# Moving transposes from TensorE to the DMA engines, with fills and port order, in a linear-attention and Fourier-mixing kernel

## The chip, the cores and the metric

One core of one Trainium2 chip runs the whole program. The metric is device time in microseconds (us), the median of several executions. An execution counts as slow when it is over 1.5% above the fastest of the same kernel. The median and the range that are given first are of all four executions; where some of the four were slow, the median of the fast ones stands beside them and is the one that is compared. Engines are called TensorE (PE in the profile), ScalarE (ACT), VectorE (DVE), GpSimd (POOL) and SyncE (SP); "PEld" is TensorE's weight load.

## The reference, cut to what matters

```python
# r, k, v, w: [4, 8, 768, 48]; u: [8, 48]; w_ch1: [384, 1536]; w_ch2: [1536, 384]; all float32
for t in range(S):                                    # recurrence over 768 steps, 8 heads
    cur = einsum('bhd,bhe->bhde', u * k_t, v_t)
    y_t = einsum('bhd,bhde->bhe', r_t, state + cur)
    state = w_t[..., None] * state + einsum('bhd,bhe->bhde', k_t, v_t)
x = y as [4, 768, 384]
u_ = x + real(fft(fft(x, axis=1), axis=2))            # Fourier mixing
un = (u_ - mean) / sqrt(var + 1e-6)
out = u_ + maximum(un @ w_ch1, 0) @ w_ch2             # MLP
```

## The kernel before

The recurrence is worked out in chunks of 128 steps: 6 chunks for each of 4 batches, so 24 chunks. In a chunk, r and k are scaled by decay factors (`rh`, `kh`, rows = time) and are then transposed (`rT`, `kT`, rows = channels), which is the form in which the matmuls that follow, which sum over channels, take them. After the Fourier mixing the normed rows `un` are transposed (`unt`) for the MLP.

```python
        # in attention(b, c), for each of 24 chunks
        def tr_r(e):
            for h in range(H):                                   # 8 heads
                o0 = 128 * h - 64 * (h % 2)
                ins = e.transpose(psb(trr)[:, 128 * h:128 * h + 128], rflat[:, o0:o0 + 128], IDB[:, :])
            return ins
        op("pe", 450, tr_r, r=["IDB", ("RH", i2)], w=[trr])
        # ... the same for k, 4 transposes ...
        op("act", 1000, lambda e: e.activation(rT[:, :, :].rearrange("p h t -> p (h t)"), psb(trr)[:, :], ACTF.Copy),
           r=[trr], w=[("RTB", i2)])
        op("act", 570, lambda e: e.activation(kT[:, :, :].rearrange("p h t -> p (h t)"), psb(trk)[:, 0:512], ACTF.Copy),
           r=[trk], w=[("KTB", i2)])
        # ... in mix(b), for each of 24 blocks of normed rows
            op("act", 600, act(un[:, :], uf[:, kb, :], ACTF.Identity, scale=-1.0, bias=agg[:, kb, 0:1]), ...)
            def tr(e, un=un, tu=tu):
                for m in range(NM):                              # 3 tiles; NIDW is the negative identity
                    ins = e.matmul(ps(tu)[:, 128 * m:128 * m + 128], un[:, 128 * m:128 * m + 128], NIDW[:, 128:256])
                return ins
            op("pe", 168, tr, r=["NIDW", ("UN", n % 3)], w=[tu])
            op("act", 475, ...)                                  # eviction of tu into unt
        # ... weights of the MLP, on GpSimd's queue
            op("pool", 1000, lambda e, q=q: e.dma_start(W1[:, q, :], moe_w_ch1[q * 128:(q + 1) * 128, :]), ...)   # x3
            op("pool", 1000, lambda e, q=q: e.dma_start(W2[:, 4 * q:4 * q + 4, :], ...), ...)                      # x3
```

`op(engine, ns, f, r=, w=)` records an operation with a cost estimate. `schedule()` is a list scheduler in Python: it simulates the engines with these estimates and priority keys (the constants `A0, AP, F0, ...`, "the plan" below) and fixes each engine's order. The program gives each engine its instructions in this order, each preceded by waits for the semaphores of what it needs, and what stands behind a held instruction waits too: in `after_wlate` below, ScalarE did nothing for 13.4 us behind two issues. So a change of an estimate, or of the work on one engine, can move instructions on all of them.

## Time and profile before

| | before |
|---|---|
| time, median of 4 (in the rounds with the kernel after) | 220.97 us (220.22 to 222.15) |
| busy over the span of 219.5 us: TensorE / VectorE / ScalarE / GpSimd | 196.0 / 155.1 / 153.0 / 119.4 us |
| mean granted TensorE clock | 0.982 |

The next fence has lines of the profile's page of the kernel before: busy time by engine; the span in 40 slices of 5.5 us (busy tenths, the granted TensorE clock in tenths, the DMA engines' busy share); the chain of work that ended last, by engine and by line; and three groups of instructions (busy us, mean ns of one, idle time before them and what ended it).

```profile
PE 196.0 (89%) x1838; PEld 130.4 (59%) x1838; DVE 155.1 (71%) x317; ACT 153.0 (70%) x322; POOL 119.4 (54%) x152
...
PE   0165798989969999999999999999999999999993
...
ACT  2349758969689885468988975689899246773330
...
PEclk9999679999999999999999999999999999999998
DMA  5999999999999999601938981015001010111102
...
PE 79%; DVE 13%; ACT 6%; issue 1%; DVEq 0%
...
L573 ACT ACTIVATE rtb<-bank 128x1024 bf16<-128x1024 bf16 x24 | 24.6, 1026 | 9.2 <-PE bank L564 8.9
...
L564 PE MATMUL bank<-idw,rh 128*128 128x128 bf16 x192 | 15.1, 223 | 5.5 <-DVE rh L552 5.5
L575 ACT ACTIVATE ktb<-bank 128x512 bf16<-128x512 bf16 x24 | 14.3, 597 | 6.0 <-PE bank L570 5.8
```

How to read it: TensorE is full from slice 13 on (from 66 us), 79% of the chain is TensorE's, and ScalarE's digits are mostly 6 to 9 up to slice 31. So TensorE bounds the kernel, with ScalarE not far behind. The DMA engines are full in the first 16 slices (some 88 us), where the inputs and weights are loaded. L573, L575 and L683 (489 ns, 24 times) are the evictions of transposes that the change removes (of L573 and L575, 18 of the 24). The view by stretch gives the numbers for the stretch that matters, 46 to 192 us (the columns are busy us and, in brackets, instructions by engine, then clock, DMA share and GB/s):

```profile
core 0: us, PE busy (x) PEld busy (x) DVE busy (x) ACT busy (x) POOL busy (x), PEclk, DMA share, GB/s
46.00:192.00 146.00, 143.60 (x1432) 98.58 (x1433) 109.54 (x234) 112.92 (x243) 85.56 (x103) 1.00 0.52 109
```

### The profile page before, as it was taken

How to read it: one execution, taken by the hardware profiler on the slowest of the kernel's cores; microseconds unless marked ns; L12 is line 12 of the kernel's file. 1: busy time of each engine (PE TensorE's matmuls, PEld its weight loads, DVE VectorE, ACT ScalarE, POOL GpSimd, SP SyncE). 2: the span in 40 equal slices, each digit the busy share in tenths (PEclk: the TensorE clock that was granted, in tenths of full speed). 3: DMA queues.
4: the chain of work that ended last, by engine and by line, in shares of the span. 5: the costliest groups of instructions: out<-in, count | busy, mean ns of one | idle time of the engine just before them, and what ended most of it. 6: DMA issues, size and time to landing. Idle time of an engine off the chain costs nothing.

```text
span 219.5 us, 4738 instructions
## 1 busy us (share of the span) xinstructions
PE 196.0 (89%) x1838; PEld 130.4 (59%) x1838; DVE 155.1 (71%) x317; ACT 153.0 (70%) x322; POOL 119.4 (54%) x152
## 2 busy tenths in 40 slices
PE   0165798989969999999999999999999999999993
PEld 0043455566637767566777776667777756656661
DVE  8967869997889886397587983975897818622322
ACT  2349758969689885468988975689899246773330
POOL 8818849787959898831389998103754130000000
PEclk9999679999999999999999999999999999999998
DMA  5999999999999999601938981015001010111102
GB/s 117 207 213 216 218 184 220 188 206 185 172 203 180 198 188 219 136 0 47 218 67 161 215 198 37 0 41 141 3 0 39 36 40 0 43 66 39 72 18 90
DMA packets 105478, 26.45 MB, mean 120 GB/s; under 512 B 100336, under 2 KB 105072, under 8 KB 105456
## 3 DMA queue, kind: packets, MB, share of 16 engines
q1 hardware_dynamic: 103440, 23.80, 51.0%
q0 software_dynamic: 2016, 2.36, 6.5%
q8 instruction: 14, 0.23, 0.4%
q14 instruction: 8, 0.07, 0.1%
HBM read 23.79 MB, written 4.72 MB: 130 GB/s over the span
## 4 chain that ended last, share of the span: by engine, by line
PE 79%; DVE 13%; ACT 6%; issue 1%; DVEq 0%
PE bank L702 21%; PE bank L721 21%; PE bank L645 7%; PE bank L661 5%; PE bank L564 4%; PE bank L583 4%; DVE xf L378 2%; DVE msk L382 2%; PE bank L612 2%; PE bank L678 2%; PE bank L570 2%; DVE ah L587 2%; PE bank L524 2%; PE bank L615 2%; PE bank L526 1%; PE bank L759 1%
## 5 line engine op out<-in xcount | busy, mean ns | idle before, releaser
L702 PE MATMUL bank<-unt,w 128*128 128x384 bf16 x288 | 56.5, 325 | 0.1
L721 PE MATMUL bank<-w,ht 128*128 128x384 bf16 x288 | 53.5, 326 | 0.0
L711 ACT ACTIVATE ht<-bank 128x384 bf16<-128x384 f32 x80 | 37.7, 499 | 19.3 <-PE bank L702 19.1
L587 DVE TENSOR_TENSOR ah<-bank,msk 128x512 bf16<-128x512 f32 x48 | 31.1, 682 | 8.3 <-PE bank L583 8.3
L721 PEld LDWEIGHTS bank<-w,ht 128*128 128x128 bf16 x288 | 26.7, 98 | 14.9 <-ACT unt L683 0.3
L702 PEld LDWEIGHTS bank<-unt,w 128*128 128x128 bf16 x288 | 26.3, 97 | 14.8 <-issue 0.2
L573 ACT ACTIVATE rtb<-bank 128x1024 bf16<-128x1024 bf16 x24 | 24.6, 1026 | 9.2 <-PE bank L564 8.9
L378 POOL TENSOR_TENSOR vtd<-in_v,dc 128x384 f32<-128x384 f32 x24 | 20.3, 848 | 16.7 <-DVE dc L544 16.7
L726 DVE SCALAR_TENSOR_TENSOR osb<-bank,rstd,uf 128x384 f32<-128x384 f32 x24 | 14.7, 614 | 18.4 <-PE bank L721 18.4
L378 POOL TENSOR_TENSOR rk<-in_r,in_k 128x384 f32<-128x384 f32 x24 | 24.4, 1020 | 0.8 <-DMA in_r<-in_r_dram 0.8
L378 POOL TENSOR_TENSOR rk<-rk,ub 128x384 f32<-128x384 f32 x24 | 24.7, 1028 | 0.2
L663 DVE TENSOR_TENSOR uf<-bank,x 128x384 f32<-128x384 f32 x24 | 12.3, 542 | 11.7 <-PE bank L661 11.7
L564 PE MATMUL bank<-idw,rh 128*128 128x128 bf16 x192 | 15.1, 223 | 5.5 <-DVE rh L552 5.5
L575 ACT ACTIVATE ktb<-bank 128x512 bf16<-128x512 bf16 x24 | 14.3, 597 | 6.0 <-PE bank L570 5.8
L378 POOL TENSOR_TENSOR xf<-x 128x191 bf16<-128x191 f32 x18 | 11.6, 644 | 12.5 <-DVE x L620 12.3
L620 DVE TENSOR_TENSOR x<-bank,vtd 128x384 f32<-128x384 f32 x24 | 13.3, 556 | 6.5 <-PE bank L615 4.6
L378 DVE TENSOR_TENSOR xf<-x 128x192 bf16<-128x192 f32 (+1 forms) x30 | 17.1, 584 | 0.2
L564 PEld LDWEIGHTS bank<-idw,rh 128*128 128x128 bf16 x192 | 12.4, 99 | 7.2 <-DVE rh L552 5.6
L612 PE MATMUL bank<-vb,ah 128*128 128x48 bf16 x192 | 15.2, 185 | 0.8 <-DVE ah L587 0.8
L583 PE MATMUL bank<-rtb,ktb 128*128 128x256 bf16 x96 | 15.4, 282 | 0.5 <-DVE ah L587 0.3
L612 PEld LDWEIGHTS bank<-vb,ah 128*128 128x128 bf16 x192 | 12.9, 97 | 4.7 <-DVE ah L587 1.8
L378 POOL TENSOR_TENSOR kh<-in_k,e_0 128x384 bf16<-128x384 f32 x8 | 8.1, 1016 | 13.6 <-ACT e_0 L537 13.6
(101 smaller groups left out, 402.0 us busy)
## 6 DMA issues: line engine op xcount, KB each, us to landing
in_w<-in_w_dram SPq DMA_DIRECT2D x24, 192.0 KB, 3.7
in_k<-in_k_dram SPq DMA_DIRECT2D x24, 192.0 KB, 3.9
in_r<-in_r_dram SPq DMA_DIRECT2D x24, 192.0 KB, 3.7
in_v<-in_v_dram SPq DMA_DIRECT2D x24, 192.0 KB, 3.7
out_dram<-osb SPq DMA_DIRECT2D x24, 192.0 KB, 1.9
w<-in_moe_w_ch_dram POOLq DMA_DIRECT2D x6, 384.0 KB, 8.2
ub<-in_u_dram SPq DMA_DIRECT2D x1, 192.0 KB, 3.7
```

The source lines that it names most:

```text
L378: return lambda e: e.tensor_tensor(out=o, in0=a, in1=b, op=f)
L564: ins = e.transpose(psb(trr)[:, 128 * h:128 * h + 128], rflat[:, o0:o0 + 128], IDB[:, :])
L573: op("act", 1000, lambda e: e.activation(rT[:, :, :].rearrange("p h t -> p (h t)"), psb(trr)[:, :], ACTF.Copy), r=[trr], w=[("RTB", i2)])
L575: op("act", 570, lambda e: e.activation(kT[:, :, :].rearrange("p h t -> p (h t)"), psb(trk)[:, 0:512], ACTF.Copy), r=[trk], w=[("KTB", i2)])
L583: ins = e.matmul(ps(ta)[:, 256 * x:256 * x + 256], kT[:, q, :], rT[:, 2 * q:2 * q + 2, :].rearrange("p h t -> p (h t)"))
L587: op("dve", 660, lambda e, hf=hf, ta=ta: e.tensor_tensor(out=ah[:, 4 * hf:4 * hf + 4, :], in0=ps(ta)[:, :].rearrange("p (h t) -> p h t", t ...
L612: ins = e.matmul(ps(ty)[:, D * h:D * h + D], ah[:, h, :], vb[:, h, :], start=True, stop=first)
L645: return e.matmul(ps(t)[:, 0:HF], xf[:, s, off:off + 128], tab[:, s, :], start=a, stop=z)
L702: ins = e.matmul(ps(t)[:, 0:384], W1[:, m, 128 * j:128 * j + 128], unt[:, m, :], start=(m == 0), stop=(m == NM - 1))
L711: op("act", 475, lambda e, j=j, t=t, ht=ht: e.activation(ht[:, j, :], ps(t)[:, 0:384], ACTF.Relu), r=[t], w=[("HT", q % 2, j)])
L721: ins = e.matmul(ps(t)[:, 0:DM], ht[:, j, 128 * x:128 * x + 128], W2[:, j, :], start=(j == 0), stop=(j == NJ - 1))
L726: op("dve", 610, lambda e, kb=kb, t=t, o=o: e.scalar_tensor_tensor(out=o[:, :], in0=ps(t)[:, 0:DM], scalar=rstd[:, kb:kb + 1], in1=uf[:, k ...
```

## The change

The intent is to relieve TensorE of work that is not arithmetic. From the second batch on, `rh` and `kh`, and in all batches the normed rows, are transposed by DMA from SBUF to SBUF, issued from ScalarE's queue: 18 + 18 + 24 = 60 issues. It also takes the fills off GpSimd, makes the scheduler assume one port for VectorE and GpSimd, sets a new plan, and negates W1 once instead of transposing with a negative identity.

```diff
-    A0, AP, F0, FL, M0, ML, P, KT, KW = 46.4, 4.2, 27.3, 10.5, 48.1, 44.3, 46.2, 26.7, 29.4
+    A0, AP, F0, FL, M0, ML, P, KT, KW = 46.1, 4.9, 47.0, 11.8, 54.9, 46.6, 36.0, 5.0, 41.9      # and XB = 1
 # scheduler: one port is assumed for GpSimd and some of VectorE's operations; a transfer from ScalarE's queue is
 # taken to hold the queue for 60 ns and to land after twice its bytes
+                    if o.port:
+                        s = max(s, port_t)
+            if o.bytes and e == "act":
+                dma_t = max(dma_t, s) + o.bytes / 200.0
+                o.end = s + o.dur + 2.0 * o.bytes / 200.0 + self.DMA_FIX
 # fills (cut)
-        op("pool", 1000, fill(RH[1][:, :, :], 0.0), w=[("RH", 1)])        # ... and seven more on GpSimd
+            zero([("RH", i)], RH[i].rearrange("p a b -> p (a b)"), 512)   # ... on ScalarE; others on VectorE
 # r and k
-        op("pe", 450, tr_r, ...)   op("pe", 225, tr_k, ...)   op("act", 1000, ...)   op("act", 570, ...)
+        if b >= XB:
+            op("act", 60, lambda e: e.dma_start_transpose(rT[:, :, :], rflat), r=[("RH", i2)], w=[("RTB", i2)],
+               sem="rT%d" % i2, nbytes=128 * 1024 * 2)
+            op("act", 60, lambda e: e.dma_start_transpose(kT[:, :, :], kflat), r=[("KH", i2)], w=[("KTB", i2)],
+               sem="kT%d" % i2, nbytes=128 * 512 * 2)
+        else:                      # batch 0 as before
 # normed rows
-            op("pe", 168, tr, r=["NIDW", ("UN", n % 3)], w=[tu])          # and the eviction on ScalarE
+            op("act", 60, lambda e, kb=kb, un=un, unt=unt: e.dma_start_transpose(
+                unt[:, :, 128 * (kb % 3):128 * (kb % 3) + 128], un[:, :]), ...)
 # weights
+        for q in range(NM):
+            op("dve", 500, ts(W1[:, q, :], W1[:, q, :], -1.0, None, ALU.mult), r=[("W1", q)], w=[("W1", q)])
 # ... other cuts: cost estimates of VectorE operations, the layout of rh, a wait that orders chunks
```

More of the change, by code (lines that the diff above doesn't have):

```diff
@@ L30 @@
     __slots__ = ("eng", "fn", "deps", "users", "dur", "key", "tile", "opens", "sem", "inc", "val",
-                 "start", "end", "nd", "idx", "clk", "bytes", "order", "waits", "ready", "last", "ready0")
+                 "start", "end", "nd", "idx", "clk", "bytes", "order", "waits", "ready", "last", "ready0", "port")
     def __init__(self, eng, fn, dur, key):
@@ L72, in op @@
         o.ready0 = 0.0
+        o.port = eng == "pool" and sem is None or getattr(fn, "port", False)
         for x in r:
@@ L107, in schedule @@
         dma_t = 0.0
+        port_t = 0.0
         for o in self.ops:
@@ L143, in schedule @@
             engt[e] = s + o.dur
-            if o.bytes:
+            if o.port:
+                port_t = s + o.dur
+            if o.bytes and e == "act":
+                dma_t = max(dma_t, s) + o.bytes / 200.0
+                o.end = s + o.dur + 2.0 * o.bytes / 200.0 + self.DMA_FIX
+            elif o.bytes:
                 dma_t = max(dma_t, s + o.dur) + o.bytes / 200.0
@@ L308, in sb @@
         return nc.alloc_sbuf_tensor(name, [128] + list(shape), dt).ap()
+    W0, WP, NW, XB = 8.0, 1.6, 24, 1
+    A0, AP, F0, FL, M0, ML, P, KT, KW = 46.1, 4.9, 47.0, 11.8, 54.9, 46.6, 36.0, 5.0, 41.9
     NIN = 5
@@ L375, in psb, with shared @@
         return BANK[t.bank].bitcast(BF16)
+    def shared(f):
+        f.port = True
+        return f
     def tt(o, a, b, f):
-        return lambda e: e.tensor_tensor(out=o, in0=a, in1=b, op=f)
+        return shared(lambda e: e.tensor_tensor(out=o, in0=a, in1=b, op=f))
     def ts(o, a, s1, s2, f0, f1=None):
         if f1 is None:
-            return lambda e: e.tensor_scalar(out=o, in0=a, scalar1=s1, scalar2=None, op0=f0)
-        return lambda e: e.tensor_scalar(out=o, in0=a, scalar1=s1, scalar2=s2, op0=f0, op1=f1)
+            return shared(lambda e: e.tensor_scalar(out=o, in0=a, scalar1=s1, scalar2=None, op0=f0))
+        return shared(lambda e: e.tensor_scalar(out=o, in0=a, scalar1=s1, scalar2=s2, op0=f0, op1=f1))
     def stt(o, a, s, b, f0, f1):
-        return lambda e: e.scalar_tensor_tensor(out=o, in0=a, scalar=s, in1=b, op0=f0, op1=f1)
+        return shared(lambda e: e.scalar_tensor_tensor(out=o, in0=a, scalar=s, in1=b, op0=f0, op1=f1))
     def fill(o, val):
@@ L420, in small_constants, with zero @@
         op("dve", 210, ts(NLE[:, :], CI[:, 128:256], 0.0, -1.0, ALU.is_ge, ALU.mult), r=["CI"], w=["NLE"])
-        op("dve", 400, ts(IDW[:, :], CI[:, :], 0.0, None, ALU.is_equal), r=["CI"], w=["IDB"])
-        op("dve", 270, fill(LB[1][:, :, :], 0.0), w=[("LB", 1)])
-        op("dve", 270, fill(LB[2][:, :, :], 0.0), w=[("LB", 2)])
-        op("pool", 580, fill(KH[0][:, :, :], 0.0), w=[("KH", 0)])
-        op("pool", 1000, fill(RH[1][:, :, :], 0.0), w=[("RH", 1)])
-        op("pool", 580, fill(KH[1][:, :, :], 0.0), w=[("KH", 1)])
-        op("pool", 1000, fill(RH[2][:, :, :], 0.0), w=[("RH", 2)])
-        op("pool", 580, fill(KH[2][:, :, :], 0.0), w=[("KH", 2)])
+        op("dve", 270, ts(IDW[:, :], CI[:, :], 0.0, None, ALU.is_equal), r=["CI"], w=["IDB"])
+        op("dve", 270, fill(KH[0][:, :, :], 0.0), w=[("KH", 0)])
+        def zero(res, flat, n):
+            op("act", 150 + n / 1.2, lambda e: e.activation(flat.bitcast(FP32), CI[:, 0:1].to_broadcast([128, n]),
+                                                            ACTF.Copy, scale=0.0), r=["CI"], w=res)
+        for i in range(1, NB):
+            zero([("LB", i)], LB[i].rearrange("p a b -> p (a b)"), 256)
+            zero([("RH", i)], RH[i].rearrange("p a b -> p (a b)"), 512)
+            zero([("KH", i)], KH[i].rearrange("p a b -> p (a b)"), 256)
         for i in range(2):
-            op("pool", 400, fill(XF[i][:, :, 0:64], 0.0), w=[("XFz", i)] + [("XFn", i)], key=i)
-            op("pool", 400, fill(XF[i][:, :, 446:512], 0.0), w=[("XFz2", i)] + [("XFo", i, c) for c in range(NC)], key=i)
-            op("pool", 120, fill(X[i][:, :, DM:DM + 4], 0.0), w=[("X", i, c) for c in range(NC)], key=i)
+            op("dve", 400, fill(XF[i][:, :, 0:64], 0.0), w=[("XFz", i)] + [("XFn", i)], key=2.0 + 20 * i)
+            op("dve", 400, fill(XF[i][:, :, 446:512], 0.0), w=[("XFz2", i)] + [("XFo", i, c) for c in range(NC)], key=2.0 + 20 * i)
+            op("dve", 100, fill(X[i][:, :, DM:DM + 4], 0.0), w=[("X", i, c) for c in range(NC)], key=2.0 + 20 * i)
     MAGIC = 12582912.0
@@ L443, in tables @@
             f, fa = TF[q][:, 0:HQ], TG[q][:, 0:HQ]
-            op("dve", 300, ts(tq[0], KI[:, :], TN[:, q:q + 1], MAGIC, ALU.mult, ALU.add),
+            op("dve", 250, ts(tq[0], KI[:, :], TN[:, q:q + 1], MAGIC, ALU.mult, ALU.add),
                r=["KI", "TN"], w=[("TQ", 0)])
-            op("dve", 300, ts(tq[1], tq[0], MAGIC, -float(S), ALU.subtract, ALU.mult),
+            op("dve", 250, ts(tq[1], tq[0], MAGIC, -float(S), ALU.subtract, ALU.mult),
                r=[("TQ", 0)], w=[("TQ", 1)])
-            op("dve", 400, stt(f, KI[:, :], TC[:, q:q + 1], tq[1], ALU.mult, ALU.add),
+            op("dve", 350, stt(f, KI[:, :], TC[:, q:q + 1], tq[1], ALU.mult, ALU.add),
                r=["KI", "TC", ("TQ", 1)], w=[("TF", q)])
-            op("dve", 400, stt(fa, f, -1.0, f, ALU.mult, ALU.max), r=[("TF", q)], w=[("TG", q)])
+            op("dve", 350, stt(fa, f, -1.0, f, ALU.mult, ALU.max), r=[("TF", q)], w=[("TG", q)])
             sins.append(act(SS[:, q, 0:HQ], f, ACTF.Sin, scale=sc))
@@ L470, in tables @@
             hi = [(n, q) for q in range(3, 6)]
-            op("dve", 450, ts(T[:, 3:6, 0:HF:2], T[:, 0:3, 0:HF:2], 1.0, None, ALU.mult), r=lo, w=[(n, "even")])
-            op("dve", 450, ts(T[:, 3:6, 1:HF:2], T[:, 0:3, 1:HF:2], -1.0, None, ALU.mult), r=lo + [(n, "even")], w=hi)
-        op("pool", 600, ts(NIDW[:, :], CI[:, :], 0.0, -1.0, ALU.is_equal, ALU.mult), r=["CI"], w=["NIDW"])
+            op("dve", 590, ts(T[:, 3:6, 0:HF:2], T[:, 0:3, 0:HF:2], 1.0, None, ALU.mult), r=lo, w=[(n, "even")])
+            op("dve", 590, ts(T[:, 3:6, 1:HF:2], T[:, 0:3, 1:HF:2], -1.0, None, ALU.mult), r=lo + [(n, "even")], w=hi)
+        op("dve", 170, ts(NIDW[:, :], IDW[:, :], -1.0, None, ALU.mult), r=["IDB"], w=["NIDW"])
         op("dve", 100, ts(CP[:, :], TC[:, 0:1], 62.5, None, ALU.is_gt), r=["TC"], w=["CP0"])
@@ L508, in weights, with rodd @@
                r=[("in", "v", 5 % NIN)], w=[("W2", q)], sem="w2_%d" % q, nbytes=512 * DM * 2)
+    def rodd(rh):
+        base = rh[:, :, :].rearrange("t (q x) c -> t q (x c)", x=2)
+        return bass.AP(base.tensor, base.offset, [list(base.ap[0]), [256, HP], [192, 2], [1, D]])
+    masked = {}
     def attention(b, c):
@@ L523, in attention @@
         tce, tci = g.tile("a"), g.tile("a")
-        op("pe", 162, lambda e: e.matmul(ps(tce)[:, 0:DM], MSK[:, :], L[:, :, 0:D]),
-           r=["MSK", ("LB", i2)], w=[tce])
+        o = op("pe", 162, lambda e: e.matmul(ps(tce)[:, 0:DM], MSK[:, :], L[:, :, 0:D]),
+               r=["MSK", ("LB", i2)], w=[tce])
+        if n >= 2:
+            o.deps.add(masked[n - 2])
         op("pe", 162, lambda e: e.matmul(ps(tci)[:, 0:DM], NLE[:, :], L[:, :, 0:D]),
@@ L552, in attention @@
         op("dve", 550, lambda e: e.tensor_tensor(
-            out=rh[:, :, 0:D], in0=ps(tce)[:, 0:DM].rearrange("t (h d) -> t h d", d=D), in1=rt[:, :, :], op=ALU.mult),
+            out=rodd(rh), in0=ps(tce)[:, 0:DM].rearrange("t (q x d) -> t q x d", x=2, d=D),
+            in1=rt[:, :, :].rearrange("t (q x) d -> t q x d", x=2), op=ALU.mult),
            r=[("in", "r", i3), tce], w=[("RH", i2)])
@@ L556, in attention @@
            r=[("in", "k", i3), ("E2", i2)], w=[("KH", i2)])
-        trr, trk = g.tile("a"), g.tile("a")
         rflat = rh[:, :, :].rearrange("t h d -> t (h d)")
         kflat = kh[:, :, :].rearrange("t h d -> t (h d)")
-        def tr_r(e):
-            for h in range(H):
-                o0 = 128 * h - 64 * (h % 2)
-                ins = e.transpose(psb(trr)[:, 128 * h:128 * h + 128], rflat[:, o0:o0 + 128], IDB[:, :])
-            return ins
-        op("pe", 450, tr_r, r=["IDB", ("RH", i2)], w=[trr])
@@ L568, in tr_k, with tr_r @@
-        def tr_k(e):
-            for h in range(HP):
-                ins = e.transpose(psb(trk)[:, 128 * h:128 * h + 128], kflat[:, 128 * h:128 * h + 128], IDB[:, :])
-            return ins
-        op("pe", 225, tr_k, r=["IDB", ("KH", i2)], w=[trk])
-        op("act", 1000, lambda e: e.activation(rT[:, :, :].rearrange("p h t -> p (h t)"), psb(trr)[:, :], ACTF.Copy),
-           r=[trr], w=[("RTB", i2)])
-        op("act", 570, lambda e: e.activation(kT[:, :, :].rearrange("p h t -> p (h t)"), psb(trk)[:, 0:512], ACTF.Copy),
-           r=[trk], w=[("KTB", i2)])
+        if b >= XB:
[4 more added lines that the diff above has]
+        else:
+            trr, trk = g.tile("a"), g.tile("a")
+            def tr_r(e):
+                for h in range(H):
+                    ins = e.transpose(psb(trr)[:, 128 * h:128 * h + 128], rflat[:, 128 * h:128 * h + 128], IDB[:, :])
+                return ins
+            op("pe", 450, tr_r, r=["IDB", ("RH", i2)], w=[trr])
+            def tr_k(e):
+                for h in range(HP):
+                    ins = e.transpose(psb(trk)[:, 128 * h:128 * h + 128], kflat[:, 128 * h:128 * h + 128], IDB[:, :])
+                return ins
+            op("pe", 225, tr_k, r=["IDB", ("KH", i2)], w=[trk])
+            op("act", 1000, lambda e: e.activation(rT[:, :, :].rearrange("p h t -> p (h t)"), psb(trr)[:, :], ACTF.Copy),
+               r=[trr], w=[("RTB", i2)])
+            op("act", 570, lambda e: e.activation(kT[:, :, :].rearrange("p h t -> p (h t)"), psb(trk)[:, 0:512], ACTF.Copy),
+               r=[trk], w=[("KTB", i2)])
@@ L586, in attention @@
             op("pe", 218, amat, r=[("KTB", i2), ("RTB", i2)], w=[ta])
-            op("dve", 660, lambda e, hf=hf, ta=ta: e.tensor_tensor(
+            masked[n] = op("dve", 660, lambda e, hf=hf, ta=ta: e.tensor_tensor(
                 out=ah[:, 4 * hf:4 * hf + 4, :], in0=ps(ta)[:, :].rearrange("p (h t) -> p h t", t=128),
@@ L624, in attention @@
         xf = XF[b % 2]
-        op("dve", 520, tt(xf[:, c, 64:256], xb[:, c, 0:192], xb[:, c, 384:192:-1], ALU.add),
+        op("dve", 350, tt(xf[:, c, 64:256], xb[:, c, 0:192], xb[:, c, 384:192:-1], ALU.add),
            r=[("X", b % 2, c)], w=[("XFe", b % 2, c)])
-        op("dve" if b == 0 else "pool", 600 if b == 0 else 750, tt(xf[:, c, 256:447], xb[:, c, 1:192], xb[:, c, 383:192:-1], ALU.subtract),
+        op("dve" if b == 0 else "pool", 350 if b == 0 else 750, tt(xf[:, c, 256:447], xb[:, c, 1:192], xb[:, c, 383:192:-1], ALU.subtract),
            r=[("X", b % 2, c)], w=[("XFo", b % 2, c)])
@@ L673, in mix @@
                r=[("UF", i, kb), ("AGG", i, kb)], w=[("UN", n % 3)])
-            tu = g.tile("f")
-            def tr(e, un=un, tu=tu):
-                for m in range(NM):
-                    ins = e.matmul(ps(tu)[:, 128 * m:128 * m + 128], un[:, 128 * m:128 * m + 128], NIDW[:, 128:256])
-                return ins
-            op("pe", 168, tr, r=["NIDW", ("UN", n % 3)], w=[tu])
             hf = kb // 3
             unt = UNT[(2 * b + hf) % 2]
-            op("act", 475, lambda e, tu=tu, kb=kb, unt=unt: e.activation(
-                unt[:, :, 128 * (kb % 3):128 * (kb % 3) + 128],
-                ps(tu)[:, 0:DM].rearrange("p (m t) -> p m t", t=128), ACTF.Copy),
-               r=[tu], w=[("UNT", (2 * b + hf) % 2, kb % 3)])
+            op("act", 60, lambda e, kb=kb, un=un, unt=unt: e.dma_start_transpose(
+                unt[:, :, 128 * (kb % 3):128 * (kb % 3) + 128], un[:, :]),
+               r=[("UN", n % 3)], w=[("UNT", (2 * b + hf) % 2, kb % 3)],
+               sem="unt%d_%d" % ((2 * b + hf) % 2, kb % 3), nbytes=128 * DM * 2)
             if kb % 3 == 2:
@@ L731, in mix @@
                    r=[("OSB", n % 3)], w=[("out", b, kb)], sem="out%d" % (n % 3), nbytes=128 * DM * 4)
-    W0, WP, NW = 8.0, 1.6, 24
-    A0, AP, F0, FL, M0, ML, P, KT, KW = 46.4, 4.2, 27.3, 10.5, 48.1, 44.3, 46.2, 26.7, 29.4
     g.key = -1.0
```

## The prediction

> **What bounds the kernel now.** The 40-slice view and the table of busy time by stretch: up to about 70 us TensorE is not full (DVE, ACT and the input loads, DMA share about 1, are). From 70 to 210 us TensorE is busy in every slice (100%), ACT about 76%, DVE about 73%. From 192 us only the last MLP runs, TensorE-bound. The chain of waits is 79% TensorE, 13% DVE, 6% ACT.
>
> **Removed.** On TensorE 18 x 12 transposes of r and k (batches 1 to 3) and 24 x 3 of normed rows, 288 of 1838 matmuls. In the order of time eight r transposes hold TensorE 0.45 us, four k ones 0.22, three of a normed row 0.17: 18 x 0.67 + 24 x 0.17 = 16 us, nearly all in the TensorE-bound stretch. On ACT, their evictions: 18 x (1.03 + 0.60) + 24 x 0.49 = 41 us.
>
> **Start.** Fills leave GpSimd. Today the two mask operations on DVE show 4.5 us each while GpSimd fills; I expect well under 1 us. But the first w lands only at 5.3 us and TensorE starts at 6.2: at most 1 us there; less crowding of DVE up to 50 us may add 2 to 4.
>
> **Added.** 60 DMA transposes on ACT's queue: 18 of 256 KB, 18 of 128 KB, 24 of 96 KB. ACT runs in order, so each issue, and each wait for rh, kh or un, stops ACT. An ordinary DMA holds SP's queue 0.37 us when nothing is queued, 0.7 to 1.1 us while loads are backed up. [...] No trace here shows a transpose yet.
>
> **The balance.** A batch costs TensorE about 46 us now, 41 after. Without evictions ACT has 28.6 us of activations per batch; 18 transposes fit under TensorE's 41 us only below 0.7 us each, and at 1.0 us ACT takes today's 46. From 46 to 192 us ACT has 113 us of work; after, 113 - 41 + 60 x h. For h = 0.5 TensorE still binds: about 203 us in total. For h = 0.9, 125 us of ACT at 93% use: 207 to 210. For h = 1.35: about 235. A transposed tile also arrives 2 to 5 us after issue (estimate: loads land in 3.7 us, stores in 1.9) instead of about 1.7 through TensorE and ACT.
>
> **Prediction.** TensorE's 16 us are real, but ACT's queue should take much of it back: 216 us, range 201 to 236. Faster by over 2%: 0.44; within 2%: 0.23; slower: 0.33.
>
> **What would show it.** Mask operations under 0.5 us; TensorE near 180 us busy with holes between 60 and 180 us; ACT's busy time down to about 115 us, with unaccounted gaps at transposes; TensorE waiting for ht, rtb/ktb or unt; more ACT and DMA in the chain. If TensorE stays solid after 65 us, the optimistic side is right.
>
> **What would make it wrong.** A transpose's issue costs ACT almost nothing (then about 200); or it holds ACT until data move, or competes with loads at 50 to 90 us so that latency exceeds what three buffers hide (then over 236).

In the balance, h is the time in us for which one issue of a transpose holds ScalarE's queue. The sum came to about 203 us for h = 0.5, 207 to 210 for 0.9 and about 235 for 1.35, and the forecast to 216 us. The three values of h stand as assumptions; the rest of the sum (113 and 41 us of ScalarE's work, 60 issues) is from the trace of the kernel before. What the prediction says of the queues is measured: in the kernel before an ordinary DMA held SyncE's queue for 0.37 us at the start (at 0.73 us), and for 0.65 to 1.86 us between 5 and 36 us, where one load followed the other and the DMA engines were full (all but two at most 1.15).

## The result, and the profile after

| | before | after |
|---|---|---|
| time, median of 4 | 220.97 us (220.22 to 222.15) | 244.13 us (243.21 to 245.15) |
| ratio of fast runs | | 1.1044 (95%: 1.0968 to 1.1119) |
| span of the profiled run | 219.5 us | 241.4 us |
| busy: TensorE / ScalarE | 196.0 / 153.0 us | 194.2 / 120.2 us |
| mean granted TensorE clock | 0.982 | 0.922 |

A ratio here is the mean time of one kernel's fast runs over the mean of the other's fast runs of the same rounds, so it is not quite the ratio of the medians quoted beside it. The kernel is 23 us slower, and the time is outside the predicted range of 201 to 236 us.

The page of the kernel after, the same lines, with the line of the DMA queue that carries the transposes (packets, MB, share of 16 engines' time) and those of the three groups of transposes (issues, median us from issue to landing):

```profile
PE 194.2 (80%) x1550; PEld 117.6 (49%) x1550; DVE 148.8 (62%) x326; ACT 120.2 (50%) x268; POOL 112.6 (47%) x140
...
PE   0878698339925969989488899798688999999994
...
ACT  6588969043431745563335764446255325445340
...
PEclk9999779955985799999979999999889999999999
DMA  6999999999999989999997999743334412150102
...
q10 hardware_dynamic: 38784, 9.44, 24.3%
...
PE 36%; DMA 19%; ACT 13%; DVE 13%; ACTq 7%; POOL 5%; issue 4%; SPq 2%; DVEq 0%; POOLq 0%
...
unt<-un ACTq DMA_TRANSPOSE x24, 3.2
rtb<-rh ACTq DMA_TRANSPOSE x18, 4.3
ktb<-kh ACTq DMA_TRANSPOSE x18, 4.3
```

The stretch from 46 to 192 us of the kernel after (columns as above):

```profile
46.00:192.00 146.00, 115.93 (x935) 69.53 (x936) 92.68 (x197) 68.50 (x160) 78.50 (x95) 0.89 0.95 163
```

TensorE has 288 instructions fewer and is busy about as long. It has holes in many slices, and in the slices with holes or just after them its granted clock is 5 to 8 tenths (5 in slices 9 and 10, in and after two slices in which TensorE is busy 3 tenths). The same instructions take longer: the two matmul lines of the MLP, 288 instructions each, 333 and 337 ns in the mean instead of 325 and 326. (A slice is 6.0 us here.) The chain has gone from 79% TensorE to 36%; 19% are DMA transfers (8% loads of v, 11% the three kinds of transposes), 7% are ScalarE's queue (ACTq), which did not occur before. The DMA engines are now full to slice 25, some 150 us, instead of 88 us.

Two readings show where to look. First, the issues of the transposes on ScalarE's queue, in the views of the lines that issue them (duration min/median/max in ns: how long the queue is held, not how long the data take, which is 3.2 to 4.3 us by the page):

```profile
L592 ACTq DMA_TRANSPOSE rtb<-rh x18: 1247/1262/1851, 53.4 to 191.6; - x18
```

```profile
L594 ACTq DMA_TRANSPOSE ktb<-kh x18: 1205/1225/1782, 54.8 to 183.3; - x18
```

```profile
L713 ACTq DMA_TRANSPOSE unt<-un x24: 1193/1202/2072, 67.3 to 216.6; - x24
```

With these medians the 60 issues hold ScalarE's queue for 18 x 1.26 + 18 x 1.23 + 24 x 1.20 = 74 us, while the evictions that they replace were worth 41 us. These 74 us are not in ScalarE's busy time, since DMA issues are not counted as busy. Second, the chain of the kernel after in order of time between 40 and 75 us (start us, us, what):

```profile
41.37 9.60 DMA in_v<-in_v_dram
...
54.81 6.61 DMA ktb<-kh
...
71.54 4.71 DMA unt<-un
```

A load of v takes 9.6 us in the chain where the median is 5.2 (3.7 in the kernel before), and then two transposes are waited for. The six weight loads were issued at 38.3 to 45.9 us before; after, they start at 28.7 us: GpSimd no longer makes the fills and comes to them sooner, and the new plan has a part in it too (without it, in pe_all_oldplan below, they start at 34.2 us).

So there were several candidates:

- A, the hold: an issue of a transpose holds ScalarE's queue for 1.20 to 1.26 us (medians), and what stands behind it in the order waits.
- B, the weight loads: the new order lets them collide with other transfers.
- C, the bytes: 9.44 MB more on the DMA engines.
- D, the latency: a transposed tile arrives 3 to 4 us after its issue.
- E, the clock: TensorE's granted clock is lower where it has holes (0.922 in the mean, 0.982 before). I took this to follow from the others, and not to be a cause by itself.

### The profile page after: what moved, and what is told of

The parts are those of the page before. It is cut to its first block, busy times and chain, and to the rows that moved or that the text cites. A ratio compares the mean times of both kernels' runs of the same rounds, so it can differ in the third digit from the quotient of the medians.

```text
span 241.4 us, 4167 instructions
## 1 busy us (share of the span) xinstructions
PE 194.2 (80%) x1550; PEld 117.6 (49%) x1550; DVE 148.8 (62%) x326; ACT 120.2 (50%) x268; POOL 112.6 (47%) x140
## 3 DMA queue, kind: packets, MB, share of 16 engines
q10 hardware_dynamic: 38784, 9.44, 24.3%
HBM read 23.79 MB, written 4.72 MB: 118 GB/s over the span
## 4 chain that ended last, share of the span: by engine, by line
PE 36%; DMA 19%; ACT 13%; DVE 13%; ACTq 7%; POOL 5%; issue 4%; SPq 2%; DVEq 0%; POOLq 0%
PE bank L732 13%; PE bank L751 12%; DMA in_v<-in_v_dram 8%; ACTq L713 6%; DMA rtb<-rh 5%; ACT un L410 4%; DMA unt<-un 3%; DMA ktb<-kh 3%; PE bank L682 3%; PE bank L620 3%; DVE ah L624 2%; DVE x L657 2%; ACT ht L741 2%; POOL rk L396 2%; SPq L419 2%
## 5 line engine op out<-in xcount | busy, mean ns | idle before, releaser
L751 PE MATMUL bank<-w,ht 128*128 128x384 bf16 x288 | 54.9, 337 | 5.0 <-ACT e_0 L568 4.0
L741 ACT ACTIVATE ht<-bank 128x384 bf16<-128x384 f32 x80 | 36.9, 489 | 33.5 <-PE bank L732 28.1
L751 PEld LDWEIGHTS bank<-w,ht 128*128 128x128 bf16 x288 | 28.1, 100 | 23.5 <-ACT e_0 L568 4.3
L756 DVE SCALAR_TENSOR_TENSOR osb<-bank,rstd,uf 128x384 f32<-128x384 f32 x24 | 14.6, 612 | 13.2 <-PE bank L751 13.2
L583 DVE TENSOR_TENSOR rh<-bank,in_r 128x384 bf16<-128x384 f32 x24 | 13.2, 548 | 12.4 <-ACT bank L559 12.3
L410 ACT ACTIVATE vb<-in_v 128x384 bf16<-128x384 f32 x24 | 12.6, 525 | 16.3 <-DMA in_v<-in_v_dram 9.9
L620 PE MATMUL bank<-rtb,ktb 128*128 128x256 bf16 x96 | 17.0, 300 | 4.0 <-ACT un L410 2.3
L410 ACT ACTIVATE un<-uf,agg 128x384 bf16<-128x384 f32 x24 | 14.2, 608 | 10.1 <-DVE agg L706 2.9
L559 ACT ACTIVATE bank<-bank 128x384 f32<-128x384 f32 x24 | 11.4, 479 | 15.7 <-PE bank L553 14.9
L737 DVE TENSOR_SCALAR ht<-bank 128x384 bf16<-128x384 f32 x16 | 8.8, 551 | 10.5 <-PE bank L732 10.4
L410 ACT ACTIVATE lb<-in_w 128x384 bf16<-128x384 f32 x24 | 12.6, 524 | 5.3 <-POOL kh L396 2.2
```

The source lines that it names most:

```text
L410: return lambda e: e.activation(o, a, f, **kw)
L583: op("dve", 550, lambda e: e.tensor_tensor(out=rodd(rh), in0=ps(tce)[:, 0:DM].rearrange("t (q x d) -> t q x d", x=2, d=D), in1=rt[:, :, :] ...
L620: ins = e.matmul(ps(ta)[:, 256 * x:256 * x + 256], kT[:, q, :], rT[:, 2 * q:2 * q + 2, :].rearrange("p h t -> p (h t)"))
L741: op("act", 475, lambda e, j=j, t=t, ht=ht: e.activation(ht[:, j, :], ps(t)[:, 0:384], ACTF.Relu), r=[t], w=[("HT", q % 2, j)])
L751: ins = e.matmul(ps(t)[:, 0:DM], ht[:, j, 128 * x:128 * x + 128], W2[:, j, :], start=(j == 0), stop=(j == NJ - 1))
L756: op("dve", 610, lambda e, kb=kb, t=t, o=o: e.scalar_tensor_tensor(out=o[:, :], in0=ps(t)[:, 0:DM], scalar=rstd[:, kb:kb + 1], in1=uf[:, k ...
```

## The experiments

All kernels are timed in 3 rounds against the kernel before (median 221.4 to 221.7 us in every session; the sessions ran on different chips, and the kernel after itself was timed beside one of 221.0 us). Those marked "wrong result" compute something else.

### First group: undo parts

**pe_all**: the kernel after with all transposes back on TensorE; fills, port order and plan stay.

```diff
-    W0, WP, NW, XB = 8.0, 1.6, 24, 1
+    W0, WP, NW, XB = 8.0, 1.6, 24, 4            # r and k: TensorE in all batches
-            op("act", 60, ... e.dma_start_transpose(unt..., un[:, :]) ...)
+            op("pe", 168, tr, ...)  op("act", 475, ...)      # as in the kernel before; W1 is not negated
```

> All transposes back on TensorE (and the weights not negated), but the moved fills, the shared-port model and the changed plan constants kept. Theory A (each DMA transpose holds ACT's queue about 1.25 us, 60 of them, 76 us, against 41 us of evictions saved): the loss goes away, 214 to 224 us, ACT no longer shows gaps without a reason. Theory B (the new plan itself is bad, above all the 8.6 us in which ACT waits for a load of v at 42 to 51 us): most of the loss stays, 232 us or more, with that hole still there. Theory C (transposes load the DMA engines and delay the loads): also 214 to 224.

Measured: 228.97 us (228.29 to 229.64), ratio 1.0345 (1.0289 to 1.0402). That is between the two numbers that were expected. Without any DMA transpose the kernel is still 7 us slower than before. So the other half of the change costs by itself, and the DMA transposes cost 15 us on top of it.

**pe_all_oldplan**: the same with the plan constants of the kernel before.

```diff
-    A0, AP, F0, FL, M0, ML, P, KT, KW = 46.1, 4.9, 47.0, 11.8, 54.9, 46.6, 36.0, 5.0, 41.9
+    A0, AP, F0, FL, M0, ML, P, KT, KW = 46.4, 4.2, 27.3, 10.5, 48.1, 44.3, 46.2, 26.7, 29.4
```

> As the run before it, with the plan constants of the kernel before. Only the moved fills, the two-part write of r and the port model differ from before. Expected by all theories: 216 to 222 us (a gain of 0 to 5 from the start). Together with the run before it this prices the plan constants alone: theory B says the difference is over 10 us, A and C under 6.

Measured: 236.74 us (233.77 to 237.41; fast ones 236.5), ratio 1.0652 (1.056 to 1.0744). All theories had expected 216 to 222, so all missed. The new plan is not at fault; with the old one it is worse. In the profile the six weight loads lie at 34 to 39 us here, and ScalarE waits once for 7.0 us for a load of v. That points to B.

**sp_issue**: all 60 transposes are issued from SyncE's queue.

```diff
-            op("act", 60, lambda e: e.dma_start_transpose(rT[:, :, :], rflat), ...
+            op("sp", 60, lambda e: e.dma_start_transpose(rT[:, :, :], rflat), ...     # and for kT, unt
```

> The changed kernel with all 60 transposes issued from SP's queue instead of ACT's, same plan constants. Theory A: ACT is relieved of 76 us, so the time falls clearly, to 215 to 230 us, though SP also has 97 loads and stores to issue. Theory C (DMA bandwidth and the 3 to 4 us of latency): the data moved and the latency are the same or worse, so 240 us or more.

Measured: 249.01 us (247.58 to 250.15), ratio 1.1268 (1.1187 to 1.1349). ScalarE is free of the holds and the time gets worse. By the numbers set beforehand this speaks for C and against A. I do not count it so. SyncE has an order of its own too: an issue there (median 1.31 us for r, at most 3.6), and its wait for the row, stand before loads, and SyncE's other waits, above all those of its stores for their results (74.6 us in the kernel after, 57.0 in the kernel before), stand before transposes. This does not clear A; it moves the hold to another queue that has work of its own.

**honest**: the scheduler is told that an issue holds ScalarE's queue for 1260 ns instead of 60.

```diff
-            op("act", 60, lambda e: e.dma_start_transpose(rT[:, :, :], rflat), ...
+            op("act", 1260, lambda e: e.dma_start_transpose(rT[:, :, :], rflat), ...  # and for kT, unt
```

> The changed kernel with the scheduler told that a transpose's issue takes ACT 1260 ns instead of 60; what is issued is the same, only the order differs. If only the plan's ignorance of the cost hurts, most of the 23 us come back: 220 to 228. If the 76 us of ACT queue are themselves too many, a better order saves less than half: 232 to 244.

Measured: 254.95 us (251.66 to 256.32; the two fast ones 252.8), ratio 1.1422 (1.1319 to 1.1525), which is above both numbers that were expected; the profiled run of this kernel is not compared. A truer estimate in the list scheduler does not find the time again; it finds a worse order.

### Second group: orders kept

In the first group the scheduler made new orders each time. From here on, the order of every engine is kept and only the named thing is altered (but for rk_merged).

**pe_all_wlate**: pe_all with the six weight loads later in GpSimd's order.

```diff
+        q = order["pool"]
+        ws = [o for o in q if o.sem is not None and o.sem[:2] in ("w1", "w2")]
+        rest = [o for o in q if o not in ws]
+        order["pool"] = rest[:32] + ws + rest[32:]
```

> The kernel with the moved fills and new plan constants and all transposes on TensorE (229 us), with one thing changed: GpSimd issues the six weight loads some 15 us later in its order; nothing else moves. Theory B (those loads start 9 us earlier than in the kernel before, because GpSimd is free sooner, and take the DMA engines from the inputs just when ACT's and TensorE's order needs chunks 8 and 9): the hole between 43 and 53 us goes, 216 to 223 us. If the plan is bad for another reason: within 2 us of 229.

Measured: 217.63 us (217.43 to 218.09), ratio 0.983 (0.979 to 0.9871). This is the fastest correct kernel, 1.7% below the kernel before: clear of noise. Six instructions moved by 4.5 to 15 us are worth 11.3 us, which shows B for the kernels without DMA transposes. The view of waits from 28 to 62 us (us in total, times, longest), first of pe_all, then of pe_all_wlate:

```profile
POOL vtd L396 <- DVE dc L573: 10.0, 1, 10.0
ACT vb L410 <- DMA in_v<-in_v_dram: 7.1, 3, 3.6
DVE rh L581 <- ACT bank L557: 7.0, 2, 5.6
```

```profile
POOL kh L400 <- ACT e L570: 6.0, 1, 6.0
ACT bank L561 <- PE bank L555: 3.2, 3, 1.4
```

ScalarE's wait for the loads of v is gone, and with it the waits behind it. The four loads of v in the window from 28 to 60 us land after 6.3 us (median) in pe_all; in pe_all_wlate no load of v takes over 4.7 us (median 3.7). So it is the transfers that collide. (GpSimd also waits 3.1 us for a load of v before its first weight load in pe_all, and no longer in pe_all_wlate; this part of the 11.3 us was not separated.) So the fills, the port order and the new plan together gain 4 us (217.6 against 221.7), and the collision that came with them takes 11.

**swap_all**: the kernel before in its own order; each transpose on TensorE goes and its eviction on ScalarE becomes the DMA transpose, in the eviction's place.

```diff
-        op("pe", 450, tr_r, ...)                                  # removed from TensorE's order
-        op("act", 1000, ... activation(rT ...)                    # its place in ScalarE's order is taken by:
+        e.dma_start_transpose(rT[:, :, :], rflat)                 # and so for kT (batches 1 to 3) and unt
```

> The kernel before with the order of every engine kept as it is, and each transpose on TensorE (r and k from batch 1, all normed rows) replaced by a DMA transpose that stands where the eviction stood in ACT's order. This is the DMA path alone, without a new plan. Theory A (ACT's queue is held 60 x 1.25 us): ACT's work from 46 to 192 us goes from 113 to 147 us, the span of that stretch: 228 to 240 us. Theory D (what hurts is latency, 3 to 6 us from issue to landing against 1.7 us, in orders that were made for less): also 235 or more, with TensorE waiting for rtb, ktb and unt. If the DMA path were good and only the new plan bad: 206 to 218 us.

Measured: 270.32 us (269.28 to 272.51), ratio 1.2215 (1.2145 to 1.2285). In an order that was made for transposes on TensorE, TensorE waited 29.0 us for k tiles (11 times) in the view of waits. The latency (D) costs much where no order makes room for it; the kernel after has such an order. The holds (A) are in this number too.

**shadow_act_tiny**: the kernel before, all its transposes kept, with 60 more DMA transposes of 32 x 128 elements on ScalarE's queue whose result nobody reads.

```diff
+        e.dma_start_transpose(scratch, rflat[0:32, 0:128])        # before the eviction of r; so for k and un
```

> The kernel before, order kept, all results as before, plus 60 tiny DMA transposes (32 rows of 128) on ACT's queue next to the evictions, whose results nobody reads. They load ACT's queue and hardly the DMA engines. Theory A: ACT's work in the stretch from 46 to 192 us goes from 113 to 188 us, so 245 us or more. Theories C and D: at most 226 us.

Measured: 236.25 us (234.46 to 236.75), ratio 1.0649 (1.0594 to 1.0704). Sixty issues of 1.10 us with next to no bytes (0.50 MB) cost 14.6 us (236.25 against 221.69). That lies between the numbers of A (245 or more) and of C and D (at most 226), so it is less than I expected of the hold: it adds up to 66 us, but an issue can run beside an activation (in the trace one issue runs from 101.90 to 103.00 us and an activation starts at 102.29), and part of it may fall where ScalarE stood still anyway (it was busy 153.0 of 219.5 us in the kernel before); how large each part is was not separated.

**shadow_sp_full**: the same with 60 transposes of full size, on SyncE's queue.

```diff
+        e.dma_start_transpose(scratch, rflat)                     # on SyncE's queue; so for k and un
```

> The kernel before, order kept, all results as before, plus the 60 DMA transposes at full size on SP's queue, into tiles that nobody reads. They load the DMA engines (9.4 MB more) and hold SP, not ACT, and nobody waits for what they bring. Theory C (transposes take DMA time from the input loads): 232 us or more. Theories A and D: at most 227 us.

Measured: 246.99 us (245.23 to 247.69), ratio 1.1137 (1.108 to 1.1193). Inconclusive: the trace shows holes of 13 to 14 us that come from my edit. ScalarE may not rewrite a normed row before the shadow that reads it has landed, and the shadow stood behind loads in SyncE's order. It says nothing on C.

### Third group: take one cost after the other away from the kernel after

All of these keep the order of the kernel after on TensorE, ScalarE, VectorE and SyncE, but for three negations of W1 on VectorE that are left out (the sign is turned in the MLP's eviction instead).

**after_wlate**: only the six weight loads later, by the same edit as in pe_all_wlate.

> The kernel after with the order of every engine kept, and only the six weight loads put later among GpSimd's instructions. If the collision of the weight loads with the input loads costs here what it cost with all transposes on TensorE (11.3 us), the time is 230 to 236 us, and the stretch from 28 to 60 us shows no wait of ScalarE for in_v of over 4 us. If the DMA transposes hide that collision (the chain is elsewhere by then), it stays at 241 us or more.

Measured: 248.68 us (246.46 to 251.38; fast ones 248.3), ratio 1.1274 (1.1189 to 1.1359). The higher number came, but not for the reason that stood with it: the time does not stay, it rises. What gained 11 us without DMA transposes costs about 4 here (against 244.1). The reason is in the timeline of ScalarE (start us, us, then the instruction):

```profile
44.76 1.33 ACTq L607 DMA_TRANSPOSE rtb<-rh  x1
...
46.19 7.43 ACTq L610 DMA_TRANSPOSE ktb<-kh  x1
...
53.65 6.47 ACTq L607 DMA_TRANSPOSE rtb<-rh  x1
60.17 0.49 ACT L583 ACTIVATE e<-bank 128x388 f32<-128x388 f32 x1 [13.40 <-issue]
```

The weight loads are issued at 44.4 to 48.4 us, and the two transposes that come next hold ScalarE's queue for 7.43 and 6.47 us instead of 1.25. ScalarE does nothing for 13.4 us. Late, the weight loads no longer collide with the loads of v; they collide with the first transposes.

**unread**: after_wlate, but TensorE reads tables that stand still in place of the transposed tiles, so nobody waits for the transposes (wrong result).

```diff
-                    ins = e.matmul(ps(ta)[...], kT[:, q, :], rT[:, 2 * q:2 * q + 2, :]...)
+                    ins = e.matmul(ps(ta)[...], kTx[:, q, :], rTx[:, 2 * q:2 * q + 2, :]...)   # views of SS, CS
+            if o.eng == "pe":
+                o.deps = {d for d in o.deps if d.tag != "D"}      # D: the transposes
```

> after_wlate, but TensorE reads tables that stand still in place of the transposed tiles; the 60 DMA transposes are still issued at the same places and at full size, and nobody waits for their data. The result is wrong on purpose. If the latency of the transposes (issue to landing, 3 to 5 us) is what costs, the time falls to 222 us or less. If the hold of ScalarE's queue (about 1.25 us for each issue) or the share of the DMA engines is what costs, it stays at 228 us or more.

Measured: 245.98 us (245.12 to 247.78), ratio 1.1122 (1.1054 to 1.119). Waiting for the data is worth 2.3 us here (fast runs), hardly more than the spread; the two long holds are the same (7.84 and 7.58 us).

**unread_tiny**: the same with 32 x 128 elements in each transpose (wrong result).

```diff
-            e.dma_start_transpose(rT[:, :, :], rflat)
+            e.dma_start_transpose(rT[:, 0, 0:32], rflat[0:32, 0:128])     # so for kT, unt
```

> unread with each of the 60 transposes cut to 32x128 elements (1.10 us of hold in an earlier run, about a twentieth of the bytes). If the bytes that the transposes move slow the loads, it is at least 5 us faster than unread; if not, within 2 us of unread.

Measured: 230.29 us (229.71 to 231.26), ratio 1.0407 (1.0357 to 1.0457). The size was worth 15.7 us. In the timeline the same three issues now hold 1.19, 1.20 and 1.25 us, with the weight loads in the same place:

```profile
44.00 1.19 ACTq L618 DMA_TRANSPOSE rtb<-rh  x1
...
45.30 1.20 ACTq L621 DMA_TRANSPOSE ktb<-kh  x1
...
46.54 1.25 ACTq L618 DMA_TRANSPOSE rtb<-rh  x1
```

**unread_none**: the same with no transpose at all (wrong result).

```diff
+        order["act"] = [o for o in order["act"] if o.tag != "D"]
```

> unread without any transpose: TensorE's transposes and ScalarE's evictions are gone and nothing stands in their place (wrong result on purpose). This is the gain that the change was after: 16 us less on TensorE than the 217.6 us of the kernel with all transposes on TensorE and late weight loads, so 199 to 207 us. If the hold of ScalarE's queue costs (60 issues of 1.1 us), unread_tiny is at least 8 us slower than this one; if the hold hides in ScalarE's idle time, the two are within 3 us.

Measured: 205.53 us (204.88 to 207.24), ratio 0.9296 (0.9237 to 0.9356). This is what free transposes would have given: 12.1 us less than pe_all_wlate, and 16.0 less than the kernel before.

### Fourth group: what was still open

**unread_now**: unread without the six weight loads; the MLP reads tables (wrong result).

```diff
+        order["pool"] = [o for o in order["pool"] if o not in wl]    # wl: the weight loads
```

> unread without the six weight loads (the MLP reads tables that stand still; wrong result on purpose). If the 16 us between unread and unread_tiny are the stall in which weight loads and transposes met, the time falls to 236 us or less and no issue of a transpose holds ScalarE's queue over 3 us. If the transposes' bytes cost all along, it stays at 241 us or more.

Measured: 231.97 us (230.72 to 234.61; fast ones 231.0), ratio 1.0475 (1.0409 to 1.0541). With the fast ones 15.0 us less than unread, and 0.7 more than unread_tiny, which is within the spread. The longest hold is 2.9 us. So the transposes' bytes (C) cost little by themselves; they cost where they meet the weight loads. The 0.7 us are a lower bound, because this kernel also reads 4.7 MB less (23.79 MB of HBM reads in unread, 19.07 here).

**after_wspread**: after_wlate with the six weight loads one by one, from about 28 to 80 us.

```diff
-        order["pool"] = rest[:32] + ws + rest[32:]
+        for x, o in sorted(zip([20, 27, 32, 36, 42, 48], ws), key=lambda z: -z[0]):
+            rest.insert(x, o)
+        order["pool"] = rest
```

> after_wlate with the six weight loads spread one by one over the stretch from about 28 to 80 us, all other orders the same (correct result). If only the burst of weight loads is at fault, 231 to 238 us; if the sum of the bytes is, 243 us or more.

Measured: 243.04 us (242.5 to 246.0), ratio 1.1009 (1.094 to 1.1078). No hold of an issue exceeds 2.4 us, but the time is at the upper number: three places of the weight loads (early 244.1, late 248.7, spread 243.0) give about the same. The weights have to be fetched somewhere in a stretch where the DMA engines are full (their share in this kernel is 1.0 to 1.3 from 28 to 100 us in the view by stretch).

**unread_wspread**: unread with the weight loads of after_wspread (wrong result). It was run with the last pair.

> unread with the six weight loads spread one by one as in after_wspread; nobody waits for transposed data (wrong result on purpose). If the 11 us between unread_now and after_wspread are the weight loads, this is at 240 us or more; if they are the wait for transposed data, at 232 to 235 us.

Measured: 239.22 us (238.71 to 239.82), ratio 1.0787 (1.0737 to 1.0838). Between the two numbers, nearer to the weight loads: they cost 8.2 us against unread_now, and waiting for transposed data costs 3.8 (243.0 against 239.2).

**unread_nop**: unread_tiny with each issue replaced by nothing but its wait: ScalarE still stops until the row to be transposed is ready (wrong result).

```diff
+            if o.tag == "D":
+                o.fn, o.sem, o.bytes = (lambda e: e.nop()), None, 0
```

> unread_tiny with each of the 60 issues replaced by nothing but its wait: ScalarE still stops at the same places until the row to be transposed is ready, and issues no DMA (wrong result on purpose). If the 25 us between unread_none and unread_tiny are the holds of the queue, this is at 205 to 210 us; if they are ScalarE's waits in a fixed order, 220 us or more.

Measured: 206.29 us (205.01 to 209.64; fast ones 205.4), ratio 0.9276 (0.9214 to 0.9337). ScalarE's waits for the rows cost nothing that can be told from noise (205.5 in unread_none). The 24.9 us between this kernel and unread_tiny are the 60 issues: the orders are the same, the data are read by nobody, and the bytes are 0.50 MB. One rival is left by the edit: in unread_tiny a row that was transposed may be rewritten only after its transpose has landed, and here there is no landing to wait for. The view of waits of unread_tiny speaks against it: down to 1.2 us, where its list ends, it has no wait for a transpose; where such a wait occurs the view shows it (in merged, below, 6.4 us of GpSimd).

How a hold reaches TensorE can be read from unread_tiny. Three issues in a row hold ScalarE from 102.87 us, the exponential `e` behind them comes 4.09 us late, and TensorE waits for it:

```profile
102.87 1.95 ACTq L741 DMA_TRANSPOSE unt<-un  x1
104.86 1.25 ACTq L621 DMA_TRANSPOSE ktb<-kh  x1
106.14 1.25 ACTq L741 DMA_TRANSPOSE unt<-un  x1
107.44 0.49 ACT L589 ACTIVATE e<-bank 128x388 f32<-128x388 f32 x1 [4.09 <-issue]
...
107.98 1.46 PE L780 MATMUL bank<-w,ht 128*128 128x384 bf16 x4 [3.96 <-ACT e L589]
```

The two pages, first unread_nop, then unread_tiny:

```profile
PE 184.6 (90%) x1550; PEld 115.4 (56%) x1550; DVE 150.2 (73%) x323; ACT 121.8 (59%) x268; POOL 112.5 (55%) x140
...
PE   0697589989769989999999999999999999999993
...
PEclk9999957999957999999999999999999999999999
```

```profile
PE 189.2 (83%) x1550; PEld 115.7 (51%) x1550; DVE 150.3 (66%) x323; ACT 120.3 (53%) x268; POOL 112.2 (49%) x140
...
PE   0868598795649799993988998897779999999994
...
PEclk9999979999776999998599999999979999999999
```

The busy times of ScalarE agree within 1.5 us, so the table of busy times hides the cause altogether. What differs is TensorE's line: nearly solid from slice 13 in the one, with holes down to 3 tenths in the other, and the deepest hole (slice 19) comes with a clock of 8 and then 5 tenths. TensorE's 1550 matmuls take 189.2 us instead of 184.6, at a mean clock of 0.948 instead of 0.967, so the clock (E) has a part in the 24.9 us; how large, beyond these 4.6 us of busy time, was not separated.

**merged**: after_wspread with r and k of a chunk in one transpose, and three normed rows in one: 26 issues for the same 9.44 MB.

```diff
-    RH = [sb("rh%d" % i, [H, 128], BF16) ...]   KH = [sb("kh%d" % i, [H, 64], BF16) ...]
+    RKH = [sb("rkh%d" % i, [12, 128], BF16) for i in range(NB)]         # r and k side by side; RKT likewise
-            e.dma_start_transpose(rT..., rflat)   e.dma_start_transpose(kT..., kflat)
+            e.dma_start_transpose(RKT[i2][:, :, :], rkflat)             # where the later of the two was
-            e.dma_start_transpose(unt[:, :, 128 * (kb % 3):...], un[:, :])          # three times in a half
+            e.dma_start_transpose(unt.rearrange("p x m t -> p (x m) t"), UN3[q]...) # once; 6 un buffers, not 3
```

> after_wspread with r and k of a chunk in one transpose and the three normed rows of a half in one: 26 issues for the same bytes (correct result). If an issue holds ScalarE's queue for about 1.25 us whatever its size, 34 issues fewer give back at least 8 us against after_wspread; if the hold grows with the size, or if waiting for the last of three rows costs as much, it is within 3 us of it.

Measured: 236.98 us (234.12 to 238.29; fast ones 236.6), ratio 1.0664 (1.0593 to 1.0736). 6.4 us better than after_wspread, so between the two numbers. A merged issue mostly holds the queue little longer than a small one, as the view of the tile shows:

```profile
L628 ACTq DMA_TRANSPOSE rkt<-rkh x18: 1291/1478/5185, 50.6 to 182.9; - x18
```

With 1.48 us for r and k together and 1.32 us for three normed rows, the 26 issues hold the queue for 37 us instead of 74. But the tile lands later (5.2 us against 4.4 for r), and TensorE waits for it: DMA rkt is 9% of this kernel's chain (in after_wspread rtb and ktb together were 11%). GpSimd now waits too, 6.4 us, until it may rewrite the tile.

**rk_merged**: r and k of a chunk in one transpose, the normed rows on TensorE, the weight loads spread; the scheduler makes the order anew.

> The scaled r and k of a chunk in one DMA transpose, 18 issues in all, the normed rows on TensorE as in the kernel before, weight loads spread (correct result). ScalarE loses 29 us of evictions for 18 holds of about 1.3 us, TensorE loses 12 us of transposes. If holds and latency stay hidden: 208 to 216 us. If the latency of the transposes (about 4 us in each chunk's chain) costs: 222 us or more.

Measured: 228.81 us (226.07 to 230.08; fast ones 228.7), ratio 1.0297 (1.0229 to 1.0366). The higher of the two numbers was the right one: DMA rkt is 20% of the chain. Even the part that replaces two evictions (1.62 us together) with one issue does not pay in this kernel as it is scheduled. The order is new and the weight loads lie elsewhere, so the distance to pe_all_wlate (217.6) is not the price of these 18 issues alone.

### The sum

| from | to | us | what it is |
|---|---|---|---|
| before 221.7 | pe_all_wlate 217.6 | -4 | fills, port order, new plan, without the collision |
| pe_all_wlate 217.6 | unread_none 205.5 | -12 | transposes and evictions gone: the gain that was sought |
| unread_none 205.5 | unread_nop 205.4 | 0 | ScalarE's waits for the rows |
| unread_nop 205.4 | unread_tiny 230.3 | +25 | 60 issues on ScalarE's queue (A) |
| unread_tiny 230.3 | unread_wspread 239.2 | +9 | full-size transposes together with the weight loads (B and C; about 1 without the weight loads) |
| unread_wspread 239.2 | after_wspread 243.0 | +4 | waiting for transposed data (D) |
| after_wspread 243.0 | after 244.1 | +1 | weight loads early instead of spread, and the W1 negations |

The steps are differences of medians of fast runs, partly from different sessions, and depend on the order in which the costs are taken away; a step of 1 us is within the noise. In the first two steps the engines' orders differ too; from unread_none on they are the same, but for the weight loads and the W1 negations. In the step from unread_tiny to unread_wspread the place of the weight loads changes too. What stays open: how much the early weight loads of the kernel after itself cost, since every other place that I tried for them made another collision; and whether some order of ScalarE would hide more of the holds. I tried only the scheduler's own.

## Why the prediction was wrong, point by point

- **What bounds the kernel, and what is removed: right.** TensorE's 16 us and ScalarE's 41 us were read from the trace. With the transposes free, TensorE was busy 181.6 us (predicted "near 180") and the time was 16.0 us below before.
- **Start: right in its sizes, as far as it was separated.** The mask operation fell from 4.5 us to 0.16 us, TensorE starts at 5.8 instead of 6.2 us, and the whole of this half, with the new plan in it, is worth 4 us ("2 to 4"). What it left out is that GpSimd, free of the fills and with the new plan, issues the weight loads 3 to 10 us earlier, where they meet the loads of v. Without DMA transposes that costs 11.3 us.
- **The hold: that it stops ScalarE was right, its size too low.** "ACT runs in order, so each issue ... stops ACT" is what the runs show: the exponential behind three issues came 4.09 us late in unread_tiny, and ScalarE did nothing for 13.4 us behind two in after_wlate. The balance "113 - 41 + 60 x h" is a sum of the right kind that leans low. Read between its own cases (207 to 210 us for 0.9, about 235 for 1.35), it gives about 220 us for the 1.10 us of a tiny issue and about 228 for the mean hold of 1.23 us (74 us by 60); these two are estimates. Without any wait for data, unread_tiny came to 230.3 us and unread_now, with issues of full size and no weight loads, to 231.0. What failed is the term h. I assumed 0.5, 0.9 and 1.35 and leaned on the middle, when no trace had shown a transpose; it is 1.10 us for 32 x 128 elements and 1.20 to 1.26 us for 96 to 256 KB. Measured, nearly all is fixed: from 32 x 128 to 128 x 1024 elements, 32 times the size, the shortest hold grew from 1.10 us (unread_tiny) to 1.25 us (the kernel after). The shortest issue of an ordinary load held its queue for 0.37 us (the kernel before).
- **The latency and the bytes: named as a risk, not counted.** "Competes with loads at 50 to 90 us" stood under what would make the prediction wrong, and no term in the balance had it. Together they cost about 12 us: 231.0 us in unread_now, 239.2 with the weight loads (unread_wspread), 243.0 with the wait for transposed data as well (after_wspread). With the right h alone the balance would still have ended inside the predicted range; these missing terms put the time outside it. The prediction had named that way out ("then over 236") without counting it.
- **TensorE "near 180 us busy with holes": half right.** The holes came, and with them a mean clock of 0.922, and the 1550 matmuls took 194.2 us; the same 1550 took 181.6 us at a clock of 0.981 in unread_none.
- **The chances.** 0.33 for slower and 0.44 for faster were the wrong way round, mostly because of h.

So the step that failed is the balance on ScalarE's queue: its term for an issue was more than a quarter too small in the middle case (0.9 for 1.23 us), and the terms for the meeting of transposes with weight loads and for waiting on transposed data were missing (8 and 4 us).

## What to carry to other kernels

Before work moves from a bound engine to a DMA, count what its issue holds of the queue that issues it, in the same unit as the work that goes: here 60 issues of 1.23 us were not free, though the profile does not show them as busy (60 tiny ones cost 24.9 us, unread_tiny against unread_nop). If an issue's hold hardly grows with its size, as here (1.48 us for r and k together in merged, 1.28 and 1.22 apart in after_wspread), make fewer and larger ones, and then look at the latency that this adds (5.2 us to landing instead of 4.4). When an engine loses work, ask which transfers it will now start sooner and what they will meet; moving six load instructions within one queue was worth 11 us here, nearly as much as the 12 us that free transposes would have given.
